# An SSM convolution and a gated MLP on one core: from staged phases with resident weights to blocks of 256 tokens woven into a streamed MLP

## The chip, the cores and the metric

The kernel runs on 1 core of one Trainium2 chip. The metric is the device time of one execution in microseconds (us). Engines are named as in the profile: PE (matmul), PEld (its weight loads), DVE (vector), ACT (scalar), POOL (GpSimd), SP (which here only issues DMAs).

## The reference

Everything is bfloat16, with S = 2048 tokens and D = 576 channels; the MLP is F = 4608 wide. `mod` are six rows of 576 numbers computed from `c` and `w_mod`.

```python
h = layernorm(x) * (1 + ca) + sa                   # x = A_q
k_shift[t] = sum_j k[t - j] * shift_k[:, j]        # 4 taps
kv = k_shift * v
y  = causal_conv(kv, ssm_k) + kv * ssm_D           # length 2048, per channel; written with FFTs
x  = x + ga * (h * y)
h  = layernorm(x) * (1 + cb) + sb
x  = x + gb * ((silu(h @ w1) * (h @ w3)) @ w2)
```

## The kernel before, in words

The work stands in phases, one behind the other.

**Modulation and transposes.** `w_mod` is fetched in 35 pieces into two buffers and multiplied with silu(c) (L139 to L150). `ssm_k` is transposed on PE (L206).

**Basis, transforms.** The convolution cuts the 2048 tokens into 4 blocks of 512. Cosine and sine tables are made on DVE and ACT (L251 to L288). `transform` (L298 to L308) multiplies them with the blocks of `ssm_k` (WR, WI) and of kv (XR, XI): each group of tokens is one matmul of 512 columns and one of 64 with the same weights. kv itself is made on DVE (L311 to L334).

**Products and inverse.** For each output block s (L370) DVE multiplies and adds the spectra of all pairs j + l = s, in pieces of 128x576 (L386 to L406), 40 pieces in all; then a matmul chain brings 128 tokens at a time back (L437 to L453), including the overlap from the block before, which is twisted by DVE first (L420 to L430). Layer norm (`_layer_norm_rows`, L33) takes two sums on ACT (L38, L39), small steps on DVE and a square root on ACT (L48). The result is transposed into `h2T` for the MLP. All of DVE's work stands ahead of the last matmuls of this phase.

**MLP.** W1, W3 and W2 (16 MB) are fetched whole into SBUF when the convolution's buffers are freed (L507 to L511), and stay. For each of 4 row blocks of 512 tokens and each of 36 slices f of 128 hidden units, PE does 5 matmuls for the gate (L533), 5 for up (L538), 5 for the output of the slice before (L545). The contraction over 576 channels is four chunks of 128 rows and one of 64, and the output's 576 channels are four of 128 and one of 64:

```python
for ct in range(CT):
    n = csz[ct]                                    # 128, 128, 128, 128, 64
    nc.tensor.matmul(G[:], W1t[:n, ct, f * P:(f + 1) * P],
                     h2T[:n, ct, r0:r0 + RB], ...)
```

ACT takes the sigmoid (L551) and copies U (L555); DVE multiplies twice (L553, L557). At a row block's end ACT scales, PE transposes back and DVE adds (L564 to L569).

The order on each engine is made by the framework's scheduler from the code's order. A DMA on a hardware queue takes one of eight semaphores in turn, and its issue waits until the DMA that held it before has landed.

## Time and profile before

| what | before |
|---|---|
| median of 3 runs (lowest, highest) | 1041.92 us (1040.35, 1043.03) |
| span of the profiled execution | 1039.3 us |
| PE busy | 771.8 us, 74%, 3400 matmuls |
| DVE busy | 494.9 us, 48%, 1464 instructions |
| ACT busy | 310.1 us, 30% |
| bytes read from HBM | 37.01 MB |
| mean granted TensorE clock | 0.895 of 2.4 GHz |

The profiled execution comes without a time of its own beside its span; the runs' median lies 2.6 us above that span. A share of busy time is an average over phases with different limits, so the windows by phase say more. PE counts as busy from a matmul's start to its modelled end, so spacing between starts, not busy time, gives the price of a matmul.

### The profile page before, as it was taken

To read this page: it belongs to the slowest core of one execution; us is meant where nothing else is said; L and a number is where in the kernel's file an instruction comes from. 1 tells how busy PE (TensorE), PEld (TensorE's weight loads), DVE (VectorE), ACT (ScalarE), POOL (GpSimd) and SP (SyncE) were. 2 spreads that over 40 slices of the span, in tenths; PEclk is the share of its full clock that TensorE was granted. 3 is DMA by queue.
4 is the path that set the end of the run, shared out by engine and by line. 5 is a ranking of instruction groups with operands and counts; after the bars stand their busy time and mean duration, and the time that the engine had idled before them with its cause. 6 is when DMAs were issued, how large, how long until landed. Compare 5 with 4: busy or idle time off the path is not lost.

```text
span 1039.3 us, 9853 instructions
## 1 busy us (share of the span) xinstructions
PE 771.8 (74%) x3400; PEld 269.6 (26%) x3400; DVE 494.9 (48%) x1464; ACT 310.1 (30%) x649; POOL 1.7 (0%) x9
## 2 busy tenths in 40 slices
PE   1454688404635317239999999999999999999996
PEld 0021244202312103003333333333333333333332
DVE  1138699699999996002232242322423223432232
ACT  0014334563140303013233243332423323433232
POOL 0000000000000000000000000000000000000000
PEclk9999999756677658559999999999999999999998
DMA  7310166100000000970000000000000000000000
GB/s 234 90 35 1 46 177 188 46 1 0 1 1 0 1 0 9 389 215 1 1 1 0 1 23 1 1 0 1 1 24 1 0 1 1 24 1 0 1 1 23
DMA packets 28449, 39.99 MB, mean 38 GB/s; under 512 B 3573, under 2 KB 26544, under 8 KB 27248
## 3 DMA queue, kind: packets, MB, share of 16 engines
q1 hardware_dynamic: 15138, 20.92, 6.5%
...
q0 software_dynamic: 144, 0.59, 0.1%
q14 instruction: 23, 0.19, 0.1%
HBM read 37.01 MB, written 2.36 MB: 38 GB/s over the span
## 4 chain that ended last, share of the span: by engine, by line
PE 58%; DVE 24%; DMA 8%; issue 8%; ACT 2%; SPq 0%; POOL 0%; ACTq 0%; POOLq 0%; DVEq 0%
PE out_acc L545 18%; PE G L533 18%; PE U L538 18%; DMA kj<-in_A_k_dram 2%; DMA W1t<-in_B_w_dram 2%; PE tr_psum L302 1%; DVE kvt L332 1%; DMA W2p<-in_B_w_dram 1%; DVE ln_t L55 1%; DMA W3t<-in_B_w_dram 1%; DVE ln_xn L52 1%; DVE acc L333 1%; PE tr_psum L568 1%; DVE ztt L396 1%; DVE zpq L428 1%
## 5 line engine op out<-in xcount | busy, mean ns | idle before, releaser
L553 DVE TENSOR_TENSOR gs<-G,sg 128x512 bf16<-128x512 f32 x144 | 99.6, 692 | 314.8 <-ACT sg L551 314.6
L533 PE MATMUL G<-h2T,W1t 128*128 128x512 bf16 (+1 forms) x720 | 200.4, 386 | 23.8 <-DMA W1t<-in_B_w_dram 23.8
L538 PE MATMUL U<-h2T,W3t 128*128 128x512 bf16 (+1 forms) x720 | 199.8, 386 | 15.1 <-ACT u L555 14.7
L545 PE MATMUL out_acc<-h,W2p 128*128 128x512 bf16 (+1 forms) x720 | 198.7, 387 | 0.0
L551 ACT ACTIVATE sg<-G 128x512 bf16<-128x512 f32 x144 | 86.0, 597 | 278.4 <-PE G L533 270.0
L555 ACT CAST u<-U 128x512 bf16<-128x512 f32 x144 | 84.2, 585 | 98.4 <-PE U L538 95.9
L437 PE MATMUL inv_psum<-ZR,cos_t 128*128 128x64 bf16 (+1 forms) x128 | 26.1, 351 | 108.6 <-DVE ZR L413 100.7
L533 PEld LDWEIGHTS <-W1t 128*128 128x128 bf16 (+1 forms) x720 | 58.2, 97 | 165.7 <-issue 114.5
L557 DVE TENSOR_TENSOR h<-gs,u 128x512 bf16<-128x512 bf16 x144 | 61.2, 425 | 79.5 <-ACT u L555 79.4
L545 PEld LDWEIGHTS <-W2p 128*128 128x128 bf16 (+1 forms) x720 | 59.8, 99 | 126.8 <-issue 93.6
L538 PEld LDWEIGHTS <-W3t 128*128 128x128 bf16 (+1 forms) x720 | 58.3, 97 | 128.5 <-issue 95.1
L148 PE MATMUL mod_psum<-wmod_t,crep 128*128 128x512 bf16 (+3 forms) x35 | 19.7, 575 | 45.4 <-DMA wmod_t<-in_w_mod_dram 25.4
L459 ACT CAST w<-inv_psum 128x576 bf16<-128x576 f32 x16 | 10.0, 631 | 114.4 <-PE inv_psum L452 114.3
L437 PEld LDWEIGHTS <-cos_t 128*128 128x128 bf16 x128 | 10.3, 114 | 121.7 <-issue 60.7
L302 PE MATMUL tr_psum<-kT,cos_t 128*128 128x512 bf16 (+1 forms) x128 | 22.9, 321 | 21.1 <-DVE cos_t L263 10.4
L469 PE MATMUL tr_psum<-ident,h2row 128*128 128x128 bf16 (+1 forms) x80 | 15.2, 256 | 26.5 <-DVE h2row L57 19.7
L569 DVE TENSOR_TENSOR xo<-x_rows,tr_psum 128x128 bf16<-128x128 bf16 (+1 forms) x80 | 17.1, 213 | 31.8 <-PE tr_psum L568 31.8
L302 PEld LDWEIGHTS <-cos_t 128*128 128x128 bf16 x256 | 18.3, 104 | 51.0 <-issue 12.5
L211 ACT COPY kT<-ktr_psum 128x128 bf16<-128x128 bf16 (+1 forms) x40 | 10.2, 255 | 57.5 <-PE ktr_psum L206 55.4
L302 PE MATMUL tr_psum<-kv_rows,cos_t 128*128 128x512 bf16 (+1 forms) x128 | 21.2, 321 | 6.2 <-DVE kv_rows L334 5.4
L38 ACT ACTIVATE ln_junk<-x_rows 128x576 bf16<-128x576 bf16 x32 | 21.7, 679 | 8.2 <-DVE x_rows L462 4.2
L302 PEld LDWEIGHTS <-sin_t 128*128 128x128 bf16 x256 | 17.6, 101 | 24.5 <-issue 10.6
...
## 6 DMA issues: line engine op xcount, KB each, us to landing
W3t<-in_B_w_dram ACTq DMA_DIRECT2D x4, 1152.0 KB, 11.3
W1t<-in_B_w_dram SPq DMA_DIRECT2D x4, 1152.0 KB, 24.6
kj<-in_A_k_dram ACTq DMA_DIRECT2D x31, 144.0 KB, 2.3
kj<-in_A_k_dram SPq DMA_DIRECT2D x30, 144.0 KB, 2.3
W2p<-in_B_w_dram SPq DMA_DIRECT2D x18, 144.0 KB, 3.9
W2p<-in_B_w_dram ACTq DMA_DIRECT2D x18, 144.0 KB, 3.9
...
```

The costliest lines, as they stand in the source:

```text
L38: nc.scalar.activation(junk[:], src, ACT.Copy, accum_out=ssum[:])
L148: nc.tensor.matmul(ps[:, :n], crep[:nn, ct, :], wt[:nn, :n], start=(ct == 0), stop=(ct == CT - 1))
L302: nc.tensor.matmul(ps[:, c0:c1], basis[:, qi, bt, :], dat[:, c0:c1], start=(qi == 0), stop=(qi == TPB - 1))
L437: nc.tensor.matmul(ps[:, c0:c1], cos_t[:, kc, r, :], ZR[:, kc, c0:c1], start=(kc == 0), stop=False)
L533: nc.tensor.matmul(G[:], W1t[:n, ct, f * P:(f + 1) * P], h2T[:n, ct, r0:r0 + RB], start=(ct == 0), stop=(ct == CT - 1))
L538: nc.tensor.matmul(U[:], W3t[:n, ct, f * P:(f + 1) * P], h2T[:n, ct, r0:r0 + RB], start=(ct == 0), stop=(ct == CT - 1))
L545: nc.tensor.matmul(out_accs[dq][:, :], W2p[:, fp, d0:d1], h3_prev[:, :], start=(fp == 0), stop=(fp == NF - 1))
L551: nc.scalar.activation(sg[:], G[:], ACT.Sigmoid)
L553: nc.vector.tensor_mul(gs[:], G[:], sg[:])
L555: nc.scalar.copy(u16[:], U[:])
L557: nc.vector.tensor_mul(h3[:], gs[:], u16[:])
L569: nc.vector.tensor_add(xos[rt][:, d0:d1], x1[:, rb * RT + rt, d0:d1], pt[:, :n])
```

## The change

The kernel is written anew as a class. What it computes stays; how it does so changes in these places:

- **Transform.** The convolution goes in 8 blocks of 256 tokens with a 512-point transform at odd frequencies, `forward`: 16 matmuls of 288 columns per block and operand, no columns of 64. The overlap of a block with its neighbour is folded into the kernel's spectrum (`V` from `W` and the `W` before, in `k_block`), so there is one inverse per block and no twisting. A block's cosine and sine parts (2 x 2 x 576) are one tile of 2304 columns, and a product of two spectra (`pair`) is five DVE instructions on such tiles, or three where it is the first of its block; 36 pairs in all. Spectra of earlier blocks are written to HBM and fetched again (`get`).
- **Layer norm.** The root is a power of -0.5 on POOL (`ln_stats`), between DVE's small steps; there is no Sqrt and so no table change on ACT. Silu comes from ACT in one step, and DVE multiplies once instead of twice (`h3`).
- **MLP.** Weights are fetched again for each of the 4 row blocks: W1 and W3 in chunks of two f (three buffers, `load_w13`, rows of 512 bytes), W2 in tiles of 6 slices x 288 columns (two buffers, rows of 576 bytes). The fifth chunk of channels is padded with zeros to 128 rows. First all 36 slices of gate and up are made (up stage, result `h3` in SBUF), then the output in two halves of 288 columns with `h3` as the weights (down stage), tokens on the partitions, without transposes.
- **Weaving.** `conv` is a generator. `conv(0)` runs alone; behind each f of the up stage of row block r two steps of `conv(r + 1)` are taken (`interleave`). It has 56, 64 and 72 steps for r + 1 = 1, 2, 3, and an up stage has room for 72.
- PSUM is one pool of four tiles of two banks for all stages.

```diff
-    BLK = 512
-    L = 2 * BLK - 1
...
-                    sg = hpool.tile([P, RB], BF16, name="sg")
-                    nc.scalar.activation(sg[:], G[:], ACT.Sigmoid)
-                    gs = hpool.tile([P, RB], BF16, name="gs")
-                    nc.vector.tensor_mul(gs[:], G[:], sg[:])
...
+B = 256
+NBLK = S // B
+H = 288
+NF = F // P
+RB = 512
+NRB = S // RB
+FC = 2
+NW13 = 3
+W2C = 6
...
+    def forward(self, basis, rhs, dst):
...
+        for e in range(2):
+            for cs in range(2):
+                ps = self.ps()
+                for cc in range(2):
+                    for h in range(2):
+                        nc.tensor.matmul(ps[:, h, 0:H], basis[:, cc, cs, e, :],
+                                         rhs[:, cc, h * H:(h + 1) * H],
+                                         start=(cc == 0), stop=(cc == 1))
+                nc.scalar.copy(dst[:, 2 * e + cs, :].rearrange("p (h d) -> p h d", h=2),
+                               ps[:, :, 0:H])
+                yield
...
+    def kv_block(self, s):
...
+        for j in (2, 1, 0):
+            nc.vector.tensor_mul(tmp[:], kh[:, 3 - j:5 - j, :], tap(j))
+            nc.vector.tensor_add(kv[:], kv[:], tmp[:])
+            yield
+        nc.vector.tensor_mul(kv[:], kv[:], vt[:])
...
+        yield
+        X = self.spec.tile([P, 4, D], BF16, name="X", tag="X")
+        yield from self.forward(self.Fb, kv, X)
...
+        if s < NBLK - 2:
+            nc.sync.dma_start(self.Xd[s], X[:].rearrange("p a d -> p (a d)"))
...
+    def k_block(self, s):
...
+        pt = self.ps((P, 2, 1024), BF16)
+        for cc in range(2):
+            for ct in range(5):
+                nc.tensor.transpose(pt[:, cc, ct * P:(ct + 1) * P], nat[:, ct, cc * P:(cc + 1) * P],
+                                    self.ident[:])
+        nc.vector.tensor_copy(kT[:], pt[:, :, 0:D])
...
+        yield
+        W = self.wprev.tile([P, 4, D], BF16, name="W", tag="W")
+        yield from self.forward(self.Fk, kT, W)
+        V = self.spec.tile([P, 4, D], BF16, name="V", tag="V")
...
+            nc.vector.tensor_add(V[:, 0:4:3, :], W[:, 0:4:3, :], Wp[:, 1:3, :])
+            nc.vector.tensor_sub(V[:, 1:3, :], W[:, 1:3, :], Wp[:, 0:4:3, :])
...
+        if s < NBLK - 1:
+            nc.sync.dma_start(self.Vd[s], V[:].rearrange("p a d -> p (a d)"))
+        yield
...
+    def pair(self, X, V, s):
...
+        first = s not in self.accs
...
+        nc.vector.tensor_mul(p1[:], X[:], V[:])
+        if not first:
+            nc.vector.tensor_add(a[:], a[:], p1[:])
+        yield
+        nc.vector.tensor_mul(p2[:, 0:4:2, :], X[:, 0:4:2, :], V[:, 1:4:2, :])
+        nc.vector.tensor_mul(p2[:, 1:4:2, :], X[:, 1:4:2, :], V[:, 0:4:2, :])
+        if not first:
+            nc.vector.tensor_add(b[:], b[:], p2[:])
+        yield
...
+    def old_products(self, r):
...
+        hold = None
+        for j in range(1, s0):
+            X = self.get("X", j)
+            if j >= 2:
+                yield from self.pair(X, hold, s1)
+            hold = self.get("V", s0 - j)
+            yield from self.pair(X, hold, s0)
+        self.V1 = hold
...
+    def ln_stats(self, src, name):
...
+            nc.scalar.activation(junk[:], src[:, i, :], ACT.Copy, accum_out=ssum[:, i:i + 1])
...
+            nc.scalar.activation(junk[:], src[:, i, :], ACT.Square, accum_out=ssq[:, i:i + 1])
...
+        nc.vector.tensor_single_scalar(mean[:], ssum[:], 1.0 / D, op=ALU.mult)
+        nc.vector.tensor_mul(var[:], mean[:], mean[:])
+        nc.vector.scalar_tensor_tensor(var[:], ssq[:], 1.0 / D, var[:], op0=ALU.mult, op1=ALU.subtract)
+        nc.vector.tensor_scalar_add(var[:], var[:], EPS)
+        nc.gpsimd.tensor_tensor(rstd[:], var[:], self.neghalf[:, 0:n], op=ALU.pow)
+        return mean, rstd
...
+    def finish_block(self, s):
...
+        za, zb = self.accs.pop(s)
...
+        nc.vector.tensor_sub(za[:, 0:4:2, :], za[:, 0:4:2, :], za[:, 1:4:2, :])
+        nc.vector.tensor_add(zb[:, 0:4:2, :], zb[:, 0:4:2, :], zb[:, 1:4:2, :])
+        yield
...
+        for cc in range(2):
+            ps = self.ps()
+            for e in range(2):
+                for cs, z in ((0, za), (1, zb)):
+                    for h in range(2):
+                        nc.tensor.matmul(ps[:, h, 0:H], self.Fb[:, e, cs, cc, :],
+                                         z[:, 2 * e, h * H:(h + 1) * H],
+                                         start=(e == 0 and cs == 0), stop=(e == 1 and cs == 1))
...
+            nc.vector.tensor_mul(ty[:].rearrange("p (h d) -> p h d", h=2), ps[:, :, 0:H],
+                                 hg[:, cc, :].rearrange("p (h d) -> p h d", h=2))
+            nc.vector.tensor_add(x1[:, cc, :], x1[:, cc, :], ty[:])
+            yield
+            m, r = self.ln_stats(x1[:, cc:cc + 1, :], "l2")
+            self.norm(row[:, cc:cc + 1, 0:D], x1[:, cc:cc + 1, :], m, r, self.cbrow, self.sbrow)
+            yield
+        pt = self.ps((P, 2, 1024), BF16)
+        for cc in range(2):
+            for ct in range(5):
+                nc.tensor.transpose(pt[:, cc, ct * P:(ct + 1) * P], row[:, cc, ct * P:(ct + 1) * P],
+                                    self.ident[:])
...
+        for cc in range(2):
+            nc.scalar.copy(hT[:, :, (2 * i + cc) * P:(2 * i + cc + 1) * P],
+                           pt[:, cc, 0:640].rearrange("p (a b) -> p a b", a=5))
+        yield
...
+    def conv(self, r):
...
+        for s in (s0, s1):
+            if s > 0:
+                self.load_x(s)
+            yield from self.kv_block(s)
+            yield from self.k_block(s)
+        if r == 0:
+            self.mod_rows()
+        yield from self.old_products(r)
...
+        if s0:
+            V0 = self.get("V", 0)
+            X0 = self.get("X", 0)
+            yield from self.pair(X[s0], V0, s0)
+            yield from self.pair(X0, V[s0], s0)
+            yield from self.gate1(s0)
+            yield from self.finish_block(s0)
+            yield from self.pair(X[s0], self.V1, s1)
+            yield from self.pair(X[s1], V0, s1)
+            yield from self.pair(X0, V[s1], s1)
+            X1 = self.get("X", 1)
+            yield from self.pair(X1, V[s0], s1)
...
+        yield from self.gate1(s1)
+        yield from self.finish_block(s1)
...
+    def load_w13(self, n):
...
+        t = self.wst[n % NW13]
...
+        for i, w in enumerate((self.w1, self.w3)):
+            nc.sync.dma_start(t[:, 5 * i:5 * i + 4, :], w[0:512, cols].rearrange("(a p) f -> p a f", p=P))
+            nc.sync.dma_start(t[0:64, 5 * i + 4, :], w[512:D, cols])
...
+    def mlp(self, r, steps):
...
+        for fc in range(NF // FC):
+            w = self.load_w13(r * (NF // FC) + fc)
+            for fi in range(FC):
+                f = fc * FC + fi
+                gu = self.ps()
+                for i in range(2):
+                    for ct in range(5):
+                        nc.tensor.matmul(gu[:, i, :], w[:, 5 * i + ct, fi * P:(fi + 1) * P],
+                                         hT[:, ct, :], start=(ct == 0), stop=(ct == 4))
+                sg = self.hp.tile([P, RB], BF16, name="sg", tag="sg")
+                nc.scalar.activation(sg[:], gu[:, 0, :], ACT.Silu)
+                u = self.hp.tile([P, RB], BF16, name="u", tag="u")
+                nc.scalar.copy(u[:], gu[:, 1, :])
+                nc.vector.tensor_mul(self.h3[:, f, :], sg[:], u[:])
+                interleave(self.rate)
+        for h in range(2):
+            accs = [self.ps() for _ in range(2)]
+            for f0 in range(0, NF, W2C):
+                w = self.w2p.tile([P, W2C, H], BF16, name="w2t", tag="w2t")
+                nc.sync.dma_start(w[:], self.w2[f0 * P:(f0 + W2C) * P, h * H:(h + 1) * H]
+                                  .rearrange("(a p) d -> p a d", p=P))
...
+                for f, t in order:
+                    nc.tensor.matmul(accs[t // 2][:, t % 2, 0:H],
+                                     self.h3[:, f0 + f, t * P:(t + 1) * P], w[:, f, :],
+                                     start=(f0 + f == 0), stop=(f0 + f == NF - 1))
+                interleave(self.rate2)
+            for t in range(4):
...
+                nc.vector.tensor_mul(g[:], accs[t // 2][:, t % 2, 0:H], self.gbrow[:, h * H:(h + 1) * H])
+                nc.vector.tensor_add(x1[:, cc, h * H:(h + 1) * H], x1[:, cc, h * H:(h + 1) * H], g[:])
...
+    def run(self):
...
+        self.rate, self.rate2 = 2, 1
+        for _ in self.conv(0):
+            pass
+        for r in range(NRB):
+            self.mlp(r, self.steps(r + 1))```

What the scheduler makes of it is shown at two places. The first is DVE in the MLP's up stage. Before, DVE has two products per f (gate by sigmoid, then by up):

```order
L557 TENSOR_TENSOR h_7593<-gs,u_7591 128x512
L553 TENSOR_TENSOR gs<-G,sg 128x512
L557 TENSOR_TENSOR h_7618<-gs,u_7616 128x512
L553 TENSOR_TENSOR gs<-G,sg 128x512
L557 TENSOR_TENSOR h_7643<-gs,u_7641 128x512
```

Now, in the up stage of the third row block, one product per f (L483) has a whole pair of spectra in front of it (`p` are the products, `za` and `zb` the sums of a block):

```order
L483 TENSOR_TENSOR h_103<-sg,u 128x512
L313 TENSOR_TENSOR zb_3967<-zb_3967,p_4179 128x2304
L306 TENSOR_TENSOR p_4205<-X,V 128x2304
L310 TENSOR_TENSOR p_4206<-X,V 128x2x576
L308 TENSOR_TENSOR za_3966<-za_3966,p_4205 128x2304
L311 TENSOR_TENSOR p_4206<-X,V 128x2x576
L483 TENSOR_TENSOR h_103<-sg,u 128x512
```

Five long instructions have moved between two of the MLP's products, and a sum stands behind a different product than its own.

The second place is SP's queue, where the MLP's weights are fetched. Before, each weight is fetched once, behind the loads of k:

```order
L326 DMA kj<-in_A_k_dram 128x576 x3
L507 DMA W1t<-in_B_w_dram 128x4608 x4
L507 DMA W1t<-in_B_w_dram 64x4608
L511 DMA W2p<-in_B_w_dram 128x576 x18
L573 DMA out_dram<-xo 128x576 x8
```

Now, in the third up stage (with the semaphores that each issue waits for; `DMAHW` and a number is the landing of the DMA eight places earlier, `wst` are chunks of W1 and W3, `X` and `V` spectra that come back from HBM):

```order
L319 DMA X<-Xd 128x2304 [waits DMAHW2_49,DVE_49]
L455 DMA wst_106<-in_B_w_dram 128x4x256 [waits DMAHW3_49,PE_49]
L456 DMA wst_106<-in_B_w_dram 64x256 [waits DMAHW4_49,PE_49]
L319 DMA V<-Vd 128x2304 [waits DMAHW5_49,DVE_49]
L455 DMA wst_106<-in_B_w_dram 128x4x256 [waits DMAHW6_49,PE_49]
L456 DMA wst_106<-in_B_w_dram 64x256 [waits DMAHW7_49,PE_49]
```

The weights' issues have moved in among those of the spectra, in one queue: a spectrum that waits for DVE holds the weights behind it.

## Rows read from the trace of the kernel before

**Rows 1.** The page: busy tenths, granted clock and GB/s in 40 slices of 26 us.

```profile
PE   1454688404635317239999999999999999999996
DVE  1138699699999996002232242322423223432232
PEclk9999999756677658559999999999999999999998
GB/s 234 90 35 1 46 177 188 46 1 0 1 1 0 1 0 9 389 215 1 1 1 0 1 23 1 1 0 1 1 24 1 0 1 1 24 1 0 1 1 23
```

**Rows 2.** Windows by phase: us, busy us of PE, PEld, DVE, ACT, POOL; clock; DMA share; GB/s.

```profile
0.00:118.00 118.00, 48.24 (x160) 14.05 (x161) 51.82 (x306) 22.10 (x70) 1.68 (x9) 1.00 0.26 79
118.00:240.00 122.00, 65.79 (x474) 32.66 (x472) 99.62 (x294) 55.21 (x126) 0.00 (x0) 0.80 0.35 98
240.00:414.00 174.00, 81.25 (x519) 39.74 (x520) 163.95 (x487) 43.85 (x133) 0.00 (x0) 0.69 0.00 1
414.00:450.00 36.00, 7.02 (x20) 2.04 (x21) 3.17 (x12) 3.11 (x11) 0.00 (x0) 0.52 1.00 352
450.00:1039.00 589.00, 569.54 (x2230) 181.12 (x2229) 176.30 (x368) 185.85 (x309) 0.00 (x0) 0.98 0.03 10
```

**Rows 3.** The page's chain that ended last, by engine.

```profile
PE 58%; DVE 24%; DMA 8%; issue 8%; ACT 2%; SPq 0%; POOL 0%; ACTq 0%; POOLq 0%; DVEq 0%
```

**Rows 4.** PE's longest waits in 240 to 414 us: total, times, longest.

```profile
PE inv_psum L437 <- DVE ZR L413: 100.7, 4, 45.1
```

**Rows 5.** Timeline of the MLP, one f: start, us, instruction [idle before it].

```profile
655.67 0.55 PEld L533 LDWEIGHTS <-W1t 128*128 128x128 bf16 x4 [0.23 <-issue]
655.67 1.36 PE L533 MATMUL G<-h2T,W1t 128*128 128x512 bf16 x5
656.64 0.09 PEld L533 LDWEIGHTS <-W1t 64*128 64x128 bf16 x1 [0.42 <-issue]
656.96 1.36 PE L538 MATMUL U<-h2T,W3t 128*128 128x512 bf16 x5
658.25 1.37 PE L545 MATMUL out_acc<-h,W2p 128*128 128x512 bf16 x5
```

**Rows 6.** Timeline of PE in a transform at full clock, 8 pairs of 512 and 64 columns.

```profile
130.83 2.12 PE L302 MATMUL tr_psum<-kT,sin_t 128*128 128x512 bf16 x16 [3.47 <-DVE WR L306]
```

**Rows 7.** Groups of instructions by form, DVE and ACT: count, busy us, mean ns, idle before.

```profile
L557 DVE TENSOR_TENSOR h<-gs,u 128x512 bf16<-128x512 bf16 x144 | 61.2, 425 | 79.5 <-ACT u L555 79.4
L399 DVE TENSOR_TENSOR ztt<-XI,WI 128x576 bf16<-128x576 bf16 x24 | 10.9, 455 | 0.0
L569 DVE TENSOR_TENSOR xo<-x_rows,tr_psum 128x128 bf16<-128x128 bf16 x64 | 14.1, 220 | 25.0 <-PE tr_psum L568 25.0
L553 DVE TENSOR_TENSOR gs<-G,sg 128x512 bf16<-128x512 f32 x144 | 99.6, 692 | 314.8 <-ACT sg L551 314.6
L41 DVE TENSOR_SCALAR ln_mean<-ln_sum 128x1 f32<-128x1 f32 x32 | 4.0, 144 | 3.4 <-ACT ln_junk L38 3.4
L38 ACT ACTIVATE ln_junk<-x_rows 128x576 bf16<-128x576 bf16 x32 | 21.7, 679 | 8.2 <-DVE x_rows L462 4.2 <-DVE ln_mean L41 4.0
L38 ACT ACTIVATION_READ_ACCUMULATOR ln_junk<-x_rows 128x1 f32 x32 | 6.0, 188 | 0.0
```

**Rows 8.** Timeline of DVE: independent instructions that follow each other.

```profile
300.17 0.45 DVE L399 TENSOR_TENSOR ztt<-XI,WI 128x576 bf16<-128x576 bf16 x1
300.53 0.45 DVE L57 TENSOR_TENSOR h2row<-ln_t,mod 128x576 bf16<-128x576 bf16 x1
```

**Rows 9.** The page's DMA issues: count, KB each, median us from issue to landing.

```profile
W1t<-in_B_w_dram SPq DMA_DIRECT2D x4, 1152.0 KB, 24.6
kj<-in_A_k_dram SPq DMA_DIRECT2D x30, 144.0 KB, 2.3
```

**Rows 10.** POOL's longest instruction on data of the program, by form.

```profile
masks.py:199 POOL TENSOR_SCALAR_AFFINE_SELECT ident<-ident 128x128 bf16<-128x128 bf16 x1 | 0.3, 304 | 0.1
```

**Rows 11.** The chain in order of time, its first DMA: start, us.

```profile
1.28 8.21 DMA shk_raw<-in_A_shift_k_dram
```

More of the change, by code (lines that the diff above doesn't have):

```diff
@@ L5 @@
 import concourse.tile as tile
-from concourse import bass_utils, mybir
+from concourse import mybir
 from concourse._compat import with_exitstack
@@ L14 @@
 ACT = mybir.ActivationFunctionType
-DEBUG_STAGE = None
-def _fold_angle_index(nc, pool, out32, x, L, tmpname="fold"):
-    q = pool.tile(list(out32.shape), F32, name=tmpname + "_q")
-    qi = pool.tile(list(out32.shape), I32, name=tmpname + "_qi")
-    nc.vector.tensor_single_scalar(q[:], x, 1.0 / L, op=ALU.mult)
-    nc.vector.tensor_copy(qi[:], q[:])
-    nc.vector.tensor_copy(q[:], qi[:])
-    nc.vector.scalar_tensor_tensor(out32, q[:], -float(L), x, op0=ALU.mult, op1=ALU.add)
-    mask = pool.tile(list(out32.shape), F32, name=tmpname + "_m")
-    nc.vector.tensor_scalar(mask[:], out32, L / 2.0, None, op0=ALU.is_gt)
-    nc.vector.scalar_tensor_tensor(out32, mask[:], -float(L), out32, op0=ALU.mult, op1=ALU.add)
-    nc.vector.tensor_scalar(mask[:], out32, -L / 2.0, None, op0=ALU.is_lt)
-    nc.vector.scalar_tensor_tensor(out32, mask[:], float(L), out32, op0=ALU.mult, op1=ALU.add)
@@ L33, in _layer_norm_rows @@
-def _layer_norm_rows(nc, pool, src, dst, onep, shift, eps_col, D, post_mul=None):
-    P = nc.NUM_PARTITIONS
-    junk = pool.tile([P, D], BF16, name="ln_junk")
-    ssum = pool.tile([P, 1], F32, name="ln_sum")
-    ssq = pool.tile([P, 1], F32, name="ln_ssq")
-    nc.scalar.activation(junk[:], src, ACT.Copy, accum_out=ssum[:])
-    nc.scalar.activation(junk[:], src, ACT.Square, accum_out=ssq[:])
-    mean = pool.tile([P, 1], F32, name="ln_mean")
-    nc.vector.tensor_single_scalar(mean[:], ssum[:], 1.0 / D, op=ALU.mult)
-    msq = pool.tile([P, 1], F32, name="ln_msq")
-    nc.vector.tensor_mul(msq[:], mean[:], mean[:])
-    var = pool.tile([P, 1], F32, name="ln_var")
-    nc.vector.scalar_tensor_tensor(var[:], ssq[:], 1.0 / D, msq[:],
-                                   op0=ALU.mult, op1=ALU.subtract)
-    std = pool.tile([P, 1], F32, name="ln_std")
-    nc.scalar.activation(std[:], var[:], ACT.Sqrt, bias=eps_col[:], scale=1.0)
-    rstd = pool.tile([P, 1], F32, name="ln_rstd")
-    nc.vector.reciprocal(rstd[:], std[:])
-    xn = pool.tile([P, D], BF16, name="ln_xn")
-    nc.vector.tensor_scalar(xn[:], src, mean[:], rstd[:],
-                            op0=ALU.subtract, op1=ALU.mult)
-    t = pool.tile([P, D], BF16, name="ln_t")
-    nc.vector.tensor_mul(t[:], xn[:], onep)
-    if post_mul is None:
-        nc.vector.tensor_add(dst, t[:], shift)
-    else:
-        t2 = pool.tile([P, D], BF16, name="ln_t2")
-        nc.vector.tensor_add(t2[:], t[:], shift)
-        nc.vector.tensor_mul(dst, t2[:], post_mul)
@@ L593 @@
 ):
-    _kernel_impl(ctx, tc, A_q, A_k, A_v, A_shift_k, A_ssm_k, A_ssm_D,
-                 B_x, B_w1, B_w3, B_w2, c, w_mod, out, debug_stage=DEBUG_STAGE)
+    _Kernel(ctx, tc, A_q.flatten_outer_dims(), A_k.flatten_outer_dims(), A_v.flatten_outer_dims(),
+            A_shift_k, A_ssm_k, A_ssm_D, B_w1, B_w3, B_w2, c.flatten_outer_dims(), w_mod,
+            out.flatten_outer_dims()).run()
 _INS = ['A_q', 'A_k', 'A_v', 'A_shift_k', 'A_ssm_k', 'A_ssm_D', 'B_x', 'B_w1', 'B_w3', 'B_w2', 'c', 'w_mod']
```

767 lines of the change are left out of this document (290 added, 477 removed).

## The prediction

> **What bounds the kernel now.** First the page's slices [rows 1]: DVE is full from slice 4 to slice 15 while PE is not, the DMA has one burst at slices 16 and 17, then PE is full to the end. The windows by phase give sizes [rows 2]: 118 us of start, 122 us of transforms, 174 us of products and inverses in which DVE is busy 164 us and PE waits (one wait for the last sum of a block, L413, comes four times and costs 100.7 us, [rows 4]), 36 us of loading the MLP's weights at 352 GB/s, and 589 us of MLP with PE busy 570 us. The chain that ended last says the same: PE 58%, DVE 24%, DMA 8% [rows 3]. So two bounds stand one behind the other, DVE for some 250 us and PE for 589 us, and each engine is idle in the other's phase.
>
> **Price of a matmul.** In the transform at full clock 4608 columns pass in 2.12 us, the last matmul's tail included [rows 6]: 0.42 ns a column, the 2.4 GHz level. By that 512 columns cost 0.215 us and 288 cost 0.121. In the MLP five matmuls take 656.96 - 655.67 = 1.29 us, not 1.08 [rows 5]. Four full weight loads follow each other in 0.55 us, but the one of 64 rows waits 0.42 us. The 0.21 us too much per five are two changes of shape at 0.11 us each, into the 64 and out. The change pads to 128 rows, so 0.215 us holds throughout. The Trainium skill ("TensorE: Matmul & The Clock Gate", the section "The mechanism" of its Part 3) says that a weight load overlaps matmuls in flight only where their row groups differ. By that all 2592 matmuls of the new MLP would pay a load as well, some 0.1 us by the 0.55 us for four, 260 us in all. The row shows the reverse: loads of one shape are hidden, the differing one waits; I take the row.
>
> **Price of a DVE step.** 128 columns cost 220 ns and 576 cost 455 [rows 7], 0.525 ns a column; independent instructions start 0.36 to 0.37 us apart at 576 [rows 8]. So 1152 columns cost 0.67 us, 2304 cost 1.28 (no row has that length; if the slope did not hold, 692 ns for 512 columns from PSUM, [rows 7], would mean up to 1.35 ns a column, which I exclude since those operands are not 16-bit). A pair is 3 x 1.28 + 2 x 0.67 = 5.2 us; the first of a block 2.6. The MLP's one product adds 0.34, its 425 ns [rows 7] less the 0.09 us by which one step overlaps the next [rows 8].
>
> **The up stages, slot by slot.** A slot is one f: 10 matmuls, 2.16 us of PE, and two steps of the next convolution. It costs what its slowest engine needs.
> - 14 slots make and transform the two new blocks. PE: 2.16 plus, per block, 32 x 0.121 and 10 transposes over 7 slots, 0.7: 2.86 us, more than DVE's 1.4. 40 us.
> - Pairs: 7, 11 and 15 for row blocks 0, 1, 2, two of them the first of a block. DVE sets 5.2 + 0.34 = 5.5 us, 3.0 for a first one: 34, 56 and 78 us.
> - 7 slots of layer norms are a chain between engines. Per 128 tokens: product from PSUM 0.76, add 0.45, two ACT sums of 0.68 + 0.19, four small steps of 0.144, POOL's power, three steps of 0.45: 4.9 us; four times 20. The two gating norms, two tiles each, 6.4 us: 13. The power is new; below, 0.144 us as DVE's smallest step, above, 1.36 us, if it waits for a long DVE step; I take 0.3, POOL's nearest row [rows 10]: 6 of them, 2. Together 35 us (small steps, sums: [rows 7]).
> - The rest, 8 and 4 and 0 slots, at 2.16: 17 and 9 us.
>
> Row blocks 0 to 2: 126, 140, 153 us. The fourth has no convolution beside it: 36 x 2.16 = 78. Sum 497.
>
> **Down stages.** 12 tiles of 24 x 0.121 = 2.9 us. Two buffers: a tile's load begins when the one before last is done. 144 KB land in 2.3 us [rows 9]; the 288 KB more at 352 GB/s [rows 2] take 0.84, with 0.3 us for wait and issue 3.4. Two tiles per 2.9 + 3.4: 3.15 us each, 38 us; four times 152. With landings twice as long it would be 4.9 us a tile and 235 us; that end stays for the range, in part.
>
> **The start.** 9.5 us to the first taps [rows 11], as before. Then mostly DVE, in order: two blocks 15, pairs 10, basis 5, modulation 4, norms 35, and the next two blocks' kv, which the scheduler draws forward, 10: 88 us with the wait for data. Before, start and transforms took 240.
>
> **What moves on the queues.** All loads go to SP's one queue in order. A fetched spectrum that waits for DVE holds the weights behind it, at most one pair of 5.5 us, and three chunks of weights are in hand, 13 us of PE work: nothing. Per chunk 576 KB in 512-byte rows need 1.7 us at 352 GB/s of 4.3: hidden; its cover goes only with landings over 8 us. ACT has per slot two steps of 0.6 and the copies, under 2 us: hidden. Between stages the last transposes and copies of a block stand ahead of the next stage: 3 x 3 us. End: last adds and the store, 4 us.
>
> **Sum**: 88 + 497 + 152 + 9 + 4 = **750 us** of span. The runs' median lies 2.6 us above the span of before; I forecast **753 us** against 1041.92. Where it goes: the MLP's own stages take 4 x (78 + 38) = 464 us instead of 589, 95 of these 125 us by the 864 changes of shape at 0.11; the load of 36 us is gone; start, transforms and products, 414 us before, leave 88 in the start and 185 in the three woven stages (419 less 3 x 78).
>
> **Rivals.**
> 1. *Slots even out.* If the buffers (four PSUM tiles, two of `sg`) let a slot's idle engine run ahead, an up stage costs its fuller engine: PE 93, DVE 79, 100, 120 us, so 93 + 100 + 120 + 78 = 391. With down stages at PE's 35 us and a start of 70 the time is 620 us. For it: the scheduler mixes a block's norms with the next one's pairs. Against: two `sg` buffers cover one pair at most, and 13 f in a row are pairs. 8%.
> 2. *The clock stays low.* In 240 to 414 us PE was busy 81 of 174 us and the granted clock was 0.69, a mix of both levels [rows 2]. The new up stages leave PE waiting in the pair slots. At 1.2 GHz a block slot costs 4.3 + 1.4 = 5.7 us (+40 a stage), a plain one 4.3 (+17, +9); pairs and norms still hide it. 753 + 146 + 10 in the start: 910 us. Against: a PE that slows is busy without gaps, as in the MLP of before, where the clock was 0.98. 6%.
> 3. *POOL waits for DVE.* The power stands between DVE's steps; where a long step runs, it may have to wait out its 1.36 us, and the norm's chain with it: 24 x 1.36 = 33 us, 786 us. No row has POOL and DVE on data together. 12%. The Trainium skill ("SBUF — State Buffer", "SBUF: two separate sides") has a rule to that effect: a DVE instruction with two SBUF inputs keeps out a GpSimd one that reads SBUF, for its whole length.
> 4. *Streaming becomes the bound; slower.* Place: SP's queue in the up stages. At most eight DMAs are under way, four per chunk, so a chunk cannot come faster than half a landing. At W1t's 24.6 us [rows 9] that is 12.3 us for each of 72 chunks: 886 + 152 + 88 + 4 = 1130 us. It decides against the change from (1042 - 244) / 72 = 11.1 us a chunk, a landing of 22 us. For it: 4 x 16 MB instead of 16. Against: W1t's 24.6 us were 1152 KB pieces queued behind each other, and 144 KB land in 2.3. 2%.
>
> That the change does not weave at all is excluded by the order: MLP products and pairs alternate on DVE.
>
> **How the numbers follow.** Forecast 72%, rivals 8, 6, 12, 2%. The range goes from 700 (half of rival 1's gain in the up stages) to 840 (rival 3 and two thirds of the down stages' upper end), and holds the forecast and rival 3, 84%. Faster by over 0.3% (what a measurement here can tell from no change, 3 us): all but rival 4, and 1% for a low clock together with long landings: 0.97; within 0.3%: 0.01; slower: 0.02.
>
> **What would show it.** Right: up stages of some 126, 140, 153 and 78 us, down stages of 38; matmuls of 512 columns 0.215 us apart and no 0.42 us waits of the loads; DVE's 2304-column steps near 1.36 us long; PE in the up stages waiting for DVE (h3's buffers), not for DMA. Wrong: a fourth up stage well over 78 us (streaming, or the price of a matmul); down stages over 45 (landings); granted clock under 0.8 in the up stages (rival 2); POOL's power of over 1 us with DVE waiting for it (rival 3).

## The result and the profile after

| | before | after |
|---|---|---|
| median of 4 runs (lowest, highest) | 1042.47 us (1040.35, 1043.46) | 752.7 us (746.82, 755.55) |
| ratio, 95% interval | | 0.7217 (0.7184 to 0.7249) |
| span of the profiled execution | 1039.3 us | 753.8 us (this run's time: 755.55) |
| PE, DVE, ACT busy | 74%, 48%, 30% | 75%, 52%, 34% |
| bytes read from HBM | 37.01 MB | 97.17 MB |
| mean granted TensorE clock | 0.895 | 0.889 |

The forecast was 753.0 us. The shares of busy time hardly moved; the slices show what did (columns as in [rows 1], now 18.8 us each):

```profile
PE   0385499549899979815969898984077889999996
DVE  5668554799301264799940134299998112221111
PEclk9867699868999989966889999995579799999999
GB/s 248 260 245 101 5 193 276 234 31 95 94 134 135 193 148 280 278 135 31 95 63 134 134 173 119 204 266 142 56 60 97 64 126 172 143 128 142 40 140 103
```

Slices are counted from 0, as in the prediction. Before, DVE was full from slice 8 to slice 14 (26 us each) while PE was at 0 to 6 tenths. Now its full stretches (slices 8 and 9, 17 to 19, 26 to 29) are shorter and PE works beside most of them; in slices 17 and 28 it all but stands (below). Bytes come in all the time. The windows by stage (columns as in [rows 2]; start, then up and down stage of each row block):

```profile
0.00:86.50 86.50, 34.04 (x202) 22.91 (x203) 61.29 (x128) 33.89 (x67) 11.38 (x27) 0.78 0.61 186
86.50:213.00 126.50, 100.91 (x487) 49.36 (x497) 78.37 (x139) 57.55 (x114) 4.22 (x5) 0.88 0.48 143
213.00:252.00 39.00, 36.18 (x289) 27.95 (x287) 4.18 (x13) 1.07 (x2) 0.00 (x0) 1.00 0.52 140
252.00:396.50 144.50, 103.75 (x491) 49.83 (x500) 100.66 (x169) 60.41 (x123) 4.61 (x6) 0.86 0.50 153
396.50:437.00 40.50, 35.97 (x288) 27.75 (x286) 4.10 (x13) 1.01 (x2) 0.00 (x0) 1.00 0.49 133
437.00:586.50 149.50, 102.09 (x484) 48.95 (x492) 113.54 (x178) 60.14 (x122) 4.07 (x5) 0.83 0.47 138
586.50:631.00 44.50, 40.23 (x297) 29.91 (x295) 5.12 (x16) 1.29 (x2) 0.54 (x1) 0.92 0.41 111
631.00:708.70 77.70, 77.28 (x354) 35.23 (x360) 16.12 (x39) 37.58 (x70) 0.00 (x0) 1.00 0.45 128
708.70:753.80 45.10, 36.53 (x289) 27.85 (x286) 5.45 (x17) 1.07 (x2) 0.00 (x0) 1.00 0.40 112
```

In the third of these up stages PE's last matmul ends at 580.5; then it waits 5.5 us for the last block's first norm ahead of the MLP, and its first matmul of the down stage starts at 586.5. The chain that ended last, by engine [rows 3]:

```profile
PE 41%; DVE 35%; DMA 15%; issue 3%; ACT 3%; POOL 2%; POOLq 0%; SPq 0%; DVEq 0%; ACTq 0%
```

PE's 58% were 603 us of chain and are 309 now; DVE's share is larger, of a shorter span. A plain slot, DVE in the fourth up stage: the products of gate and up follow each other at 2.16 us, ten matmuls at 0.216, and no load waits between them (before: 1.29 us per five and a wait of 0.42, [rows 5]).

```profile
649.45 0.42 DVE L483 TENSOR_TENSOR h<-sg,u 128x512 bf16<-128x512 bf16 x1 [1.73 <-ACT u L482]
651.61 0.42 DVE L483 TENSOR_TENSOR h<-sg,u 128x512 bf16<-128x512 bf16 x1 [1.73 <-ACT u L482]
```

A pair slot, DVE in the third up stage, from one product to the next without a gap: 509.42 - 503.94 = 5.48 us.

```profile
503.94 0.42 DVE L483 TENSOR_TENSOR h<-sg,u 128x512 bf16<-128x512 bf16 x1
504.28 1.35 DVE L313 TENSOR_TENSOR zb<-zb,p 128x2304 bf16<-128x2304 bf16 x1
505.55 1.35 DVE L306 TENSOR_TENSOR p<-X,V 128x2304 bf16<-128x2304 bf16 x1
506.81 0.75 DVE L310 TENSOR_TENSOR p<-X,V 128x1152 bf16<-128x1152 bf16 x1
507.48 1.35 DVE L308 TENSOR_TENSOR za<-za,p 128x2304 bf16<-128x2304 bf16 x1
508.75 0.75 DVE L311 TENSOR_TENSOR p<-X,V 128x1152 bf16<-128x1152 bf16 x1
509.42 0.42 DVE L483 TENSOR_TENSOR h<-sg,u 128x512 bf16<-128x512 bf16 x1
```

The down stage: PE runs 48 matmuls, two tiles of W2, and waits for the landing of the third.

```profile
219.46 6.04 PE L496 MATMUL ps<-w2t,h 128*128 128x288 bf16 x48 [0.54 <-DMA w2t<-in_B_w_dram]
225.97 0.77 PE L496 MATMUL ps<-w2t,h 128*128 128x288 bf16 x5 [0.47 <-DMA w2t<-in_B_w_dram]
```

### The profile page after: what moved, and what is told of

It reads as the page before. It is cut to its first block, busy times and chain, and to the rows that moved or that the text cites. A ratio compares the mean times of both kernels' runs of the same rounds, so it can differ in the third digit from the quotient of the medians.

```text
span 753.8 us, 8712 instructions
## 1 busy us (share of the span) xinstructions
PE 567.0 (75%) x3163; PEld 319.7 (42%) x3201; DVE 388.8 (52%) x708; ACT 254.0 (34%) x503; POOL 24.8 (3%) x44
## 2 busy tenths in 40 slices
PE   0385499549899979815969898984077889999996
DVE  5668554799301264799940134299998112221111
## 4 chain that ended last, share of the span: by engine, by line
PE 41%; DVE 35%; DMA 15%; issue 3%; ACT 3%; POOL 2%; POOLq 0%; SPq 0%; DVEq 0%; ACTq 0%
PE ps L477 24%; PE ps L496 11%; DMA w2t<-in_B_w_dram 10%; DVE zb L313 5%; DVE za L308 4%; PE ps L230 4%; DVE p L306 4%; DVE h L483 2%; DVE p L311 2%; DVE p L310 2%; DMA V<-Vd 2%; POOL l2r L351 2%; DVE xn L366 1%; DVE xn L364 1%; DVE kvt L249 1%
## 5 line engine op out<-in xcount | busy, mean ns | idle before, releaser
L477 PE MATMUL ps<-h2T,wst 128*128 128x512 bf16 x1402 | 340.9, 398 | 12.4 <-ACT u L482 6.2
L477 PEld LDWEIGHTS <-wst 128*128 128x128 bf16 x1440 | 146.5, 102 | 186.6 <-issue 36.8
L480 ACT ACTIVATE sg<-ps 128x512 bf16<-128x512 f32 x144 | 85.9, 596 | 364.6 <-PE ps L477 277.0
L496 PE MATMUL ps<-w2t,h 128*128 128x288 bf16 x1152 | 149.4, 289 | 15.0 <-DMA w2t<-in_B_w_dram 14.8
L483 DVE TENSOR_TENSOR h<-sg,u 128x512 bf16<-128x512 bf16 x144 | 60.8, 423 | 156.4 <-ACT u L482 156.4
L496 PEld LDWEIGHTS <-h 128*128 128x128 bf16 x1152 | 113.5, 99 | 50.3 <-issue 14.5
L504 DVE TENSOR_TENSOR og<-ps,gbrow 128x288 bf16<-128x288 f32 x32 | 13.2, 452 | 143.4 <-PE ps L496 143.4
L482 ACT CAST u<-ps 128x512 bf16<-128x512 f32 x144 | 83.7, 581 | 0.0
L306 DVE TENSOR_TENSOR p<-X,V 128x2304 bf16<-128x2304 bf16 x28 | 37.9, 1352 | 0.1
L313 DVE TENSOR_TENSOR zb<-zb,p 128x2304 bf16<-128x2304 bf16 x28 | 37.8, 1352 | 0.0
L308 DVE TENSOR_TENSOR za<-za,p 128x2304 bf16<-128x2304 bf16 x28 | 37.8, 1351 | 0.0
L230 PE MATMUL ps<-kT,Fk 128*128 128x288 bf16 x128 | 22.0, 317 | 16.4 <-DVE kT L272 14.8
L233 ACT CAST W<-ps 128x576 bf16<-128x576 f32 x32 | 19.8, 654 | 20.2 <-PE ps L230 20.1
```

What stands on the lines that cost most here:

```text
L230: nc.tensor.matmul(ps[:, h, 0:H], basis[:, cc, cs, e, :], rhs[:, cc, h * H:(h + 1) * H], start=(cc == 0), stop=(cc == 1))
L233: nc.scalar.copy(dst[:, 2 * e + cs, :].rearrange("p (h d) -> p h d", h=2), ps[:, :, 0:H])
L306: nc.vector.tensor_mul(p1[:], X[:], V[:])
L308: nc.vector.tensor_add(a[:], a[:], p1[:])
L313: nc.vector.tensor_add(b[:], b[:], p2[:])
L477: nc.tensor.matmul(gu[:, i, :], w[:, 5 * i + ct, fi * P:(fi + 1) * P], hT[:, ct, :], start=(ct == 0), stop=(ct == 4))
```

## The experiments

The theory tested: the change gains in three parts, each bound by what the forecast says (no more changes of shape on PE, lighter DVE work, DVE laid beside PE), and what is left open are slots in which DVE is the slower engine, norms' chains, and W2's landings. The runs came in three groups, each beside its own runs of the kernel before (medians 1038.5 to 1040.7 us), so ratios to before are compared; "against the change" is the difference of the ratio to 0.7217, times 1042.5 us.

| run | time, us | ratio to before, 95% | against the change |
|---|---|---|---|
| b1_before_pad | 955.19 | 0.9181 (0.9163 to 0.9200) | |
| e1_rows64 | 784.46 | 0.7529 (0.7500 to 0.7558) | +33 |
| e2_noweave | 862.97 | 0.8300 (0.8273 to 0.8327) | +113 |
| e3_w2b3 | 730.78 | 0.7028 (0.6995 to 0.7060) | -20 |
| e5_nopairs | 640.00 | 0.6161 (0.6140 to 0.6183) | -110 |
| e6_nopow | 732.12 | 0.7050 (0.7036 to 0.7064) | -17 |
| e7_double | 764.46 | 0.7360 (0.7340 to 0.7379) | +15 |
| e8_hp3 | 750.66 | 0.7215 (0.7194 to 0.7235) | 0 |
| e9_mix | 722.19 | 0.6940 (0.6917 to 0.6964) | -29 |
| e10_spread | 686.76 | 0.6600 (0.6575 to 0.6625) | -64 |
| s7_mix_spread12_w3 | 647.96 | 0.6242 (0.6229 to 0.6255) | -102 |
| e11_best | 638.05 | 0.6127 (0.6103 to 0.6151) | -114 |

### Padding, taken out of the change and put into the kernel before

```diff
# e1_rows64, in the change
-                        nc.tensor.matmul(gu[:, i, :], w[:, 5 * i + ct, fi * P:(fi + 1) * P],
-                                         hT[:, ct, :], ...
+                        nc.tensor.matmul(gu[:, i, :], w[:n, 5 * i + ct, fi * P:(fi + 1) * P],
+                                         hT[:n, ct, :], ...      # n = 128, 128, 128, 128, 64
# b1_before_pad, in the kernel before (W1t, W3t, h2T, W2p zeroed by POOL, W2p 640 columns wide)
-                        n = csz[ct]
+                        n = P
...
-                                         W2p[:, fp, d0:d1],
+                                         W2p[:, fp, dq * P:(dq + 1) * P],
```

> The fifth chunk of channels goes back to 64 rows in the up stage (zeros no longer multiplied). Theory: each group of five matmuls then pays two changes of shape at 0.11 us, as in the MLP of before, 0.43 us per f. It is open where PE sets the slot: the fourth up stage goes from 78 to 93 us, the 14 block slots and the 8, 4 and 0 plain slots of the others lose 0.43 us each; pair slots hide it. Sum 16 + 18 + 5 = +39 us, about 792 us. Rival (the Trainium skill, 'TensorE: Matmul & The Clock Gate', 'The mechanism': a load overlaps the matmul in flight only where row groups differ): the differing chunk costs nothing and may even hide its load, 753 us or less, fourth up stage 78 or less.

> The kernel before with one part of the change alone: the 64-row chunk of gate and up and the 64-column chunk of the output are padded with zeros to 128. Theory: 0.21 us per group of five go away, 432 groups, 91 to 95 us, the MLP's 589 us become some 495, the whole 947 to 952 us; no load waits 0.42 us any more. Rival (the page's rule that equal row groups do not overlap): no gain, 1042 us, or up to 0.1 us more for each of the 864 padded chunks.

e1: 33 us more, where 39 were expected; the fourth up stage takes 92.8 us (from 648.1 to 740.9), 93 expected, and the three woven ones lose 5.5 to 7 us each, 19 us in all instead of 23. PE's weight loads there:

```profile
670.00 0.55 PEld L478 LDWEIGHTS <-wst 128*128 128x128 bf16 x4 [0.23 <-issue]
670.97 0.09 PEld L478 LDWEIGHTS <-wst 64*128 64x128 bf16 x1 [0.42 <-issue]
671.29 0.55 PEld L478 LDWEIGHTS <-wst 128*128 128x128 bf16 x4 [0.23 <-issue]
```

Five matmuls are 671.29 - 670.00 = 1.29 us again, with the wait of 0.42 that the change had removed. b1: the kernel before falls by 8.2%, 85 us, where 91 to 95 were expected (2.6 us of the difference is that its MLP gets under way later, at 463.4 instead of 460.8 us; the rest was not followed). PE in its MLP, five by five:

```profile
600.71 1.24 PE L551 MATMUL out_acc<-h,W2p 128*128 128x512 bf16 x5
601.79 1.24 PE L538 MATMUL G<-h2T,W1t 128*128 128x512 bf16 x5
602.87 1.24 PE L544 MATMUL U<-h2T,W3t 128*128 128x512 bf16 x5
```

1.08 us per five. In both kernels the multiplication by zeros is cheaper than the narrower chunk. The Trainium skill says, in its list of what overlaps, that a load overlaps matmuls in flight only where row groups differ ("TensorE: Matmul & The Clock Gate", "The mechanism"). These traces do not agree: equal loads are hidden, and the differing one costs 0.2 us per five.

### Without weaving

```diff
-        self.rate, self.rate2 = 2, 1
+        self.rate, self.rate2 = 0, 0
```

> No step of the next convolution is taken inside the MLP's loops; conv(r+1) is written behind the whole mlp(r), and only what the scheduler draws forward overlaps. Theory: weaving is the part that lays DVE beside PE, so the up stages fall to 78 us each and three convolutions of some 85, 105 and 125 us stand in the open: 88 + 4 x 78 + 4 x 41 + 315 + 4 = 883 us, less what the scheduler overlaps at the seams: 840 to 890. Rival: most of the gain is the cheaper transform, the one-product MLP and the padding, and weaving is worth little since each pair slot lasts as long as its DVE work anyway: under 790 us.

113 us more: 863 us, within the 840 to 890 expected. The three convolutions, now between the MLPs (columns as above):

```profile
203.80:283.70 79.90, 22.14 (x137) 13.96 (x135) 65.29 (x111) 24.25 (x52) 4.32 (x6) 0.62 0.35 120
402.90:503.20 100.30, 23.04 (x137) 14.56 (x136) 86.11 (x131) 24.34 (x52) 5.58 (x6) 0.61 0.35 120
622.20:735.30 113.10, 22.13 (x137) 14.22 (x135) 98.91 (x136) 21.17 (x44) 4.89 (x5) 0.61 0.25 82
```

They take 293 us in the open, DVE busy 250 of them, and the three up stages fall to about 80 us each. Woven, the up stages with the wait behind the third took 126.5 + 144.5 + 149.5 - 3 x 77.7 = 187 us beyond three plain ones. With b1 the gain can be split along a path of measured kernels: padding 85 us (1 to 0.918), the lighter convolution, the single product and the streamed load 92 us (to 0.830), weaving 113 us (to 0.722). What the 92 us are made of was not taken apart.

### DVE's products, and more buffers

```diff
# e5_nopairs
         first = s not in self.accs
+        if not first:
+            yield
+            yield
+            return
# e8_hp3
-        self.hp = pool("hp", bufs=2)
+        self.hp = pool("hp", bufs=3)
```

> Leaves out the products of all but the first pair of each block (28 of 36 pairs; the spectra are still fetched). Theory: a pair slot lasts as long as DVE's 5.5 us and falls to PE's 2.16; 5, 9 and 13 such slots in the three woven up stages, 17, 30 and 43 us less (about 110, 114 and 100 us), and 5 us in the start: 95 us in all, about 658 us; the granted clock rises above 0.93. Rival: the stages are long for another reason (the norms' chains, the half clock, PSUM), DVE's products mostly lie beside that: less than 45 us, over 708 us.

> A third buffer for the up stage's sg and u. Theory: the pairs stand in a row on DVE, up to 8 slots of 5.5 us behind each other, and a third buffer moves only the edge of that row: 748 to 757 us. Rival 1 of the prediction (buffers let the slots even out): the woven up stages go toward the fuller engine, 105 to 120 us instead of 127 to 144, 690 us or less.

e5: 110 us less, 95 expected. The woven up stages are 107.5, 104.7 and 100.6 us, 19, 40 and 43 less against 17, 30 and 43 expected; the granted clock in them, 0.83 to 0.88 before, is 0.95 to 1.00. So DVE's products do set their slots; they do not lie beside other waits. e8: nothing, the woven up stages are 125.5, 144.3 and 142.9 us. One more buffer of `sg` and `u` does not even the slots out; up to 8 slots of 5.5 us stand behind each other on DVE, more than two or three f can cover. Rival 1 as it was put, with the buffers as they are, is refuted by the change's own up stages, 126 to 144 us instead of 93 to 120. More PSUM tiles were not tried.

### The power on POOL

```diff
-        nc.vector.tensor_scalar_add(var[:], var[:], EPS)
-        nc.gpsimd.tensor_tensor(rstd[:], var[:], self.neghalf[:, 0:n], op=ALU.pow)
+        nc.vector.tensor_scalar_add(rstd[:], var[:], EPS)
```

> Leaves out POOL's power (the inverse root becomes variance plus epsilon, one DVE step as before). Theory: each of the 24 norms' chains is shorter by the power's 0.7 to 0.8 us and two hand-overs, about 1.0 us; it is open in the start (6 norms, some in parallel) and where a stage waits for the last norm, beside PE's work elsewhere: 6 to 12 us less, 741 to 747 us. Rival (POOL waits for long DVE steps): 24 times 1.4 us or more, 30 us less, 722 us.

17 us less, between the two expectations: neither number held. By the profiles the start falls by 5 us, the three woven up stages with the gap behind them by 5, 7 and 2; each of these numbers is uncertain by some 2 us (the start is 83.7 to 87.3 us in e3, e8, e10 and s7, which leave it as it is). In all it is 0.7 us for each of the 24 norms, so nearly all of them were open, and not only some. The change's own trace says the same: DVE idles for the power 23 times, 15.6 us in all (total, times, longest):

```profile
DVE xn L364 <- POOL l2r L351: 9.5, 16, 0.7
DVE xn L364 <- POOL l1r L351: 6.1, 7, 0.9
```

Alone the power takes 0.54 us for one tile, and 1.52 beside a long product:

```profile
358.03 1.35 DVE L306 TENSOR_TENSOR p<-X,V 128x2304 bf16<-128x2304 bf16 x1
358.26 1.52 POOL L351 TENSOR_TENSOR l2r<-l2v,neghalf 128x1 f32<-128x1 f32 x1 [4.55 <-DVE l2v L350]
...
583.79 0.54 POOL L351 TENSOR_TENSOR l2r<-l2v,neghalf 128x1 f32<-128x1 f32 x1 [6.43 <-DVE l2v L350]
```

DVE's product ends at 359.38 and POOL at 359.78, 0.40 us later. The same distance of 0.40 stands behind the end of DVE's instruction in all seven of the change's powers that began beside a DVE instruction on two SBUF inputs (five of 0.93 to 1.52 us among them). The Trainium skill ("SBUF — State Buffer", "SBUF: two separate sides") says that such an instruction keeps GpSimd out for its whole length; the trace agrees, with 1.52 against 0.54 us. So rival 3's mechanism is real, but it met 7 of 24 powers and made them longer by 3 x 0.98 + 0.51 + 0.39 + 2 x 0.08 = 4.0 us in all, not 33. DVE lost nothing by it: it idles 0.43 to 0.44 us behind these seven, for its long step runs meanwhile, and 0.7 to 0.9 behind most of the others.

### W2's third buffer, and the streaming doubled

```diff
# e3_w2b3
-        self.w2p = pool("w2p", bufs=2)
+        self.w2p = pool("w2p", bufs=3)
# e7_double, in load_w13 (twice[0], twice[1]: two tiles 128x4x256)
         for i, w in enumerate((self.w1, self.w3)):
+            nc.sync.dma_start(self.twice[i][:], w[0:512, cols].rearrange("(a p) f -> p a f", p=P))
```

> A third buffer for W2's tiles. Theory: in the down stage every second tile waits 0.7 to 0.9 us for a landing that began when the tile before last was done; with a third buffer a landing has two tiles' time (5.9 us against 3.5) and the waits go. The four down stages fall from 39 to 45 us to about 35 (the third a few us more, its start is at half clock), in all 16 to 22 us: 731 to 737 us. Rival: the queue's own pace or PE's price sets the 3.3 us per tile; a third buffer then changes under 5 us.

> The four large weight DMAs of every chunk pair are doubled: each 128x4x256 piece of W1 and W3 is fetched a second time into a tile that nobody reads, 36 MB of reads more per 37 MB of those weights. Theory: streaming is hidden; a chunk of six DMAs with eight under way and landings of 3.4 to 4 us needs some 3 us of the 4.3 that PE takes: at most 8 us more, under 761 us; fourth up stage 78 to 80. Rival: streaming is near its bound: the fourth up stage grows by 20 us or more, the whole to over 790 us.

e3: 20 us less. Its down stages (columns as above):

```profile
209.30:244.60 35.30, 35.30 (x290) 28.20 (x289) 4.19 (x13) 1.07 (x2) 0.00 (x0) 1.00 0.57 155
...
568.80:608.60 39.80, 39.04 (x296) 29.98 (x295) 5.12 (x15) 1.29 (x2) 0.55 (x1) 0.90 0.45 123
```

35.3 us is 288 matmuls at 0.1226: PE without a wait (the second and the fourth are 35.3 too). The third begins behind PE's 6 us of idling, at a lower clock (0.90 over its window), and takes 4.5 us more.

e7: 15 us more, where at most 8 were expected and 20 in the fourth up stage would have spoken for rival 4. That stage is 77.7 us, as in the change; the loss lies in the first two down stages (39.0 and 40.5 us in the change; the other two are no longer than there):

```profile
208.50:256.60 48.10, 38.46 (x290) 28.84 (x289) 4.20 (x13) 1.07 (x2) 0.00 (x0) 0.96 0.90 249
399.50:446.60 47.10, 39.51 (x290) 29.48 (x288) 4.20 (x13) 1.07 (x2) 0.00 (x0) 0.93 0.56 155
```

In the whole run PE waits 22.7 us for W2's tiles, against 14.8. That would follow if, with two buffers, whatever lands beside W2's tiles is waited for. There is a second way: the doubled fetches of one weight share a tile, and SP's queue, which W2's fetches go through as well, stands 20.1 us of the first of these stages (2.6 of the second) until the fetch before has landed in it. The two were not told apart. Beside PE's plain work streaming has room for double the large pieces.

### Order and rate: versions that beat both

```diff
# e9_mix: old products alternate with the steps that make the new blocks
+        gens = [blocks(), self.old_products(r)]      # blocks(): the loop over s0, s1 as it was
+        while gens:
+            for g in list(gens):
+                if next(g, None) is None and g.gi_frame is None:
+                    gens.remove(g)
+                else:
+                    yield
...
-        yield from self.old_products(r)
# e10_spread: steps of conv(r + 1) less 12, evenly over the 36 f; 12 in the down stage
-                interleave(self.rate)
+                want = (f + 1) * self.upsteps(r) // NF
+                interleave(want - done)
+                done = want
# s7_mix_spread12_w3: both, and three W2 buffers
# e11_best: as s7, 18 steps for the down stage, two per tile of W2
```

> Order alone: the products of old spectra (1, 5 and 9 pairs) alternate step by step with the steps that make the new blocks; two steps per f as before, two W2 buffers. Theory: a slot with one block step and half a pair costs DVE 3.3 us; 18 such slots replace 9 block slots of 2.86 and 9 pair slots of 5.5 in the third woven stage (75 to 59), 10 replace 5 and 5 in the second (42 to 33), 2 us in the first: 27 us less, about 726 us. Rival: a slot lasts as long as both its parts (chains through PSUM), no gain: 745 us or more.

> Rate alone: the next convolution's steps are spread over all 36 f, and its last 12 (the last five half pairs and the last block's norms) are taken in the down stage, one per W2 tile; order of the steps and two W2 buffers as in the change. Theory: of each woven up stage 5 x 2.6 us of DVE and the 20 us of the second block's norms leave for the down stage, in which DVE is idle, and PE's plain work fills the rest: 15 to 25 us less per woven stage, down stages up to 5 us longer: 680 to 705 us. Rival: the down stages grow by what the up stages lose: 740 us or more.

> A version by the theory: DVE's work is laid more evenly beside PE's. The products of old spectra alternate with the steps that make the new blocks; the steps of the next convolution are spread over all 36 f of the up stage (1.2, 1.4 and 1.7 per f in place of 2), 12 of them go to the down stage, one per tile of W2; three buffers for W2. Theory: some 30 us of DVE's 50 to 110 us leave each woven up stage for a down stage in which DVE is idle, and block slots take products beside them: up stages of some 95, 105 and 115 us, down stages of 36 to 44, 630 to 665 us, granted clock above 0.93. Rival: what leaves the up stage only lengthens the down stage (two of four PSUM tiles are its sums, and the norms' chain then ends behind it): 700 us or more.

> Order, rate and third W2 buffer together, with 18 steps left for the down stage and two per tile of W2, so that the last norm ends before the down stage does. Theory: the 2 to 3.4 us in which PE waited between stages go, and the up stages lose another 6 steps of DVE: 625 to 640 us. Rival: PE's own work with its 86 us of start is the floor already (567 us would be it), or the norms' chain now ends behind the down stage: 645 us or more.

Order alone gives 29 us, 27 expected, though not stage by stage: e9's woven up stages are 129.3, 129.1 and 124.6 us, 3 more, 15 less and 19 less, where 2, 9 and 16 less were expected. Rate alone gives 64: e10's woven up stages are 103.9, 115.3 and 128.9 us, and its down stages, 40.2 to 40.9 us of matmuls, are no longer than the change's. With the third buffer the two give 102 together, in s7, somewhat less than the sum (29 + 64 + 20 = 113). s7's three woven up stages are 102, 109 and 107 us and the down stages behind them about 37.5. e11 is the fastest, 638 us, 39% under the kernel before. Its slices:

```profile
PE   0347269999988899899889879899978989999997
DVE  5679842625789944925799955995499831211111
```

Its expectation held for the whole and missed for the parts: the three woven up stages are 88.6, 88.9 and 92.2 us, better than thought, but the down stages 46 to 47, and 4.4 to 6.7 us stand before them, in which PE makes inverses and waits for DVE (each window with that time):

```profile
174.40:225.40 51.00, 43.18 (x341) 32.86 (x341) 46.71 (x91) 12.88 (x30) 5.57 (x5) 0.97 0.50 145
314.30:369.20 54.90, 43.38 (x342) 33.13 (x342) 51.84 (x100) 13.00 (x31) 5.19 (x5) 0.94 0.60 178
461.40:515.20 53.80, 44.42 (x342) 33.30 (x342) 44.34 (x86) 12.97 (x30) 4.82 (x5) 0.94 0.39 102
```

DVE's 47 and 52 us in the first two windows now exceed PE's 43, and in the third both are at 44: by these sums, some of what left the up stages has become the down stages' bound. The version with all 36 pairs (0.6127) is as fast as the change without 28 of them (0.6161), with W2's third buffer besides; what the pairs still cost in it was not run.

## Why the prediction was right

**The sum**, term by term, by the profile against 753.8 us: start 86.5 for 88; up stages 126.5, 144.4, 143.4, 77.9 for 126, 140, 153, 78 (492 for 497); down stages 39.2, 41.0, 44.5, 40.8 for 4 x 38 (165.5 for 152); hand-overs 6 for 9, all of them behind the third up stage; end 4.4 for 4 (stages from first matmul to the end of the last, neighbours overlapping by 0.2 us). Errors of -1.5, -5, +13.5 and -3 us offset each other. That the forecast of 753 met the median of 752.7 so closely is luck: one term alone was 13.5 us off, and the change's own four runs lie 8.7 us apart. The parts of the start were not compared; DVE is busy 61.3 of its 86.5 us.

**Right in mechanism and size.** A matmul of 512 columns 0.216 us (0.215), of 288 columns 0.122 (0.121), a pair slot 5.48 us (5.5), DVE's 2304 columns 1.27 us start to start (1.28) and 1.35 long (1.36), the landing of W2 3.5 us (3.4), 0.11 us per change of shape (e1's fourth stage, 92.8 for 93). Each came from rows of the kernel before, though it had no step of 2304 or matmul of 288 columns.

**Right in the sum, wrong in the parts: the woven up stages.** Each window cut where its first pair begins:

```profile
86.50:135.60 49.10, 45.38 (x236) 23.34 (x241) 23.39 (x39) 24.98 (x46) 0.00 (x0) 0.94 0.67 201
135.60:213.00 77.40, 55.52 (x253) 26.02 (x257) 54.99 (x100) 32.56 (x68) 4.22 (x5) 0.85 0.36 106
252.00:304.70 52.70, 46.07 (x237) 23.53 (x241) 25.52 (x49) 27.64 (x54) 0.70 (x1) 0.94 0.72 218
304.70:396.50 91.80, 57.69 (x255) 26.30 (x259) 75.14 (x120) 32.77 (x69) 3.92 (x5) 0.81 0.38 116
437.00:488.60 51.60, 46.68 (x249) 24.27 (x252) 19.55 (x41) 28.72 (x56) 0.70 (x1) 0.97 0.55 166
488.60:586.50 97.90, 55.41 (x236) 24.67 (x240) 94.00 (x137) 31.42 (x66) 3.38 (x4) 0.76 0.42 124
```

The part before the pairs took 49, 53 and 52 us where "14 block slots at 2.86" said 40: PE waits there for the transposed kernel (3 to 6 us a stage), the first pair of the third stage waits for a spectrum's landing (5.2 us on the chain, 2.0 of them DVE's idling), and PE makes one to three f more than 14 in the meantime. The rest took 77, 92 and 98 us, the third with the wait behind it, where pairs, norms and plain slots stood for 86, 100 and 113. The step that failed is "7 slots of layer norms ... 35" as a term of its own: the scheduler lays the first block's norms among the second block's pairs, and in the third stage DVE is busy 94 of 98 us. So +9, +13, +12 us stand against -9, -8, -15.

PE does less beside the pairs than the forecast's picture says. In the third stage one inverse matmul stands in its queue until DVE has the last sum of the first block, and four f made ahead, the four PSUM tiles, are all that DVE has meanwhile. Of PE's waits in 488.6 to 586.5 us, the longest:

```profile
PE ps L384 <- DVE za L374: 25.4, 2, 23.7
```

The granted clock is 0.76 in that window, and 0.51, the lower level, from 512 to 550 us, where PE is busy 12 of 38 us and DVE all 38. This costs nothing as long as DVE is full; in e11's order the same wait is 4.6 us at most.

**Right in mechanism, wrong in size.**
- *Down stages, 3.15 us a tile.* The forecast had 3 us a stage for waiting. Against e3's stages, which have three buffers and no wait, the landings cost 3.9, 5.7, 4.7 and 5.5 us, 20 instead of 12, since some waits were 1.9 us long; the other 4.5 us are the third stage's low clock at its start (0.50 from 586.5 to 591 us).
- *POOL's power, 0.3 us.* It is 0.54 us for one tile, 0.70 for two, and up to 1.52 behind DVE; e6 gives 0.7 us for each of 24, 17 us, where the sum had some 8. The bound of 1.36 us held for all but three, which took 1.52.

**The rivals.** 1 (slots even out) did not happen, nor with one more buffer (e8), but the time it named, 620 us, was nearly reached by ordering the steps (638 us). 2 (low clock): the clock did fall, to 0.83 to 0.88 in the woven stages, but mostly where DVE was full, and the forecast's reason against it, that a slower PE is busy without gaps, is not what the trace shows there. 3 (POOL waits for DVE) is true at seven places and small. 4 (streaming) did not come: beside PE's plain work there is room for double the large pieces (e7), but little in the down stages.
